# Staging buffers of two kinds, pair sums spread over two groups, and a later start of preparation, in a fused attention and gated-MLP kernel

## The chip, the cores and the metric

The kernel runs on one core of a Trainium2 chip. The metric is the device time of one execution in microseconds (us), and a kernel's time is the median of its runs. The engines are named as in the profile: PE (TensorE, the matrix engine), PEld (its weight loads), DVE (VectorE), ACT (ScalarE), POOL (GpSimd) and SP (SyncE), which here issues nearly all DMAs. Each engine works through its own instructions in a fixed order. A later instruction of the same engine cannot pass one that waits.

## The reference

```python
def _A_ref(x, k_cache, v_cache, wq, wo):          # attention, 32 query heads on 16 K/V heads
    W = min(4096, max(256, Sk // 4))              # 512 cached keys
    q = (x @ wq).reshape(B, Sq, Hq, Dh)...
    k, v = the last W rows of the caches, repeated for 2 query heads
    p = softmax(einsum("bhqd,bhkd->bhqk", q, k) * Dh ** -0.5)
    return einsum("bhqk,bhkd->bhqd", p, v)... @ wo
def _B_ref(x, w1, w3, w2):                        # gated MLP
    return (silu(x @ w1) * (x @ w3)) @ w2
mod = (silu(c) @ w_mod)                           # six vectors sa, ca, ga, sb, cb, gb
h = layernorm(x) * (1 + ca) + sa
x = x + ga * _A_ref(h, ...)
h = layernorm(x) * (1 + cb) + sb
return x + gb * _B_ref(h, ...)
```

There are 2048 rows x of width 576, heads of 128, an MLP width of 4608, and everything is fp32.

## The kernel before, in words

**Precision.** Every operand of a matmul is split into a high part (an ACT cast to the matrix engine's fp32r format, 128 rows wide) and a low part (the difference, taken by POOL or DVE). A product is three matmuls: high x high, high x low, low x high. The helper `split` (lines 84 and 85) does this for most operands.

**Attention** runs in 128 slots. A slot is one head with one block of 512 rows, and has four steps t = 0 to 3. In each step PE gets, in this order: transposes of the previous slot's probabilities (line 335), scores (315 to 317), a part of the next slot's query projection (266, and 274 for the last chunk), the output projection of the slot before the previous one (282). At a slot's end come the value products (351 to 353). Per step ACT makes `p` (line 325) and `pth` (336), DVE `nm` (319), `ptl` (342) and `acc` (366). A query weight `wq` of a head is loaded (`wraw`, line 215), and split into the pair `wh`, `wl` two slots ahead of use. Pairs live in the eight buffers of tag `w`, and serve two slots.

**The MLP** follows in 72 groups, 36 for each pair of row blocks. A group is 7 products (`product`, line 570) of sums of operand blocks, a two-level scheme that does with 7 products what 8 blocks would ask for. They are named p1 to p7 and run in the order p1, p2, p6, p7, p5, p3, p4, steps k = 0 to 6 of a group. Group g belongs to d = g // 2 (d = 0 to 35), j = g % 2. Between the products stand `down` units: 14 for each d, seven a group, run in the two groups after it (`multiply`, line 648; DVE adds each result to its sum, line 636). They use p1 to p7 activations that `act_steps` makes and splits (`split_act`), step by step. The last group but one takes all 14 of d = 34, and d = 35 uses `plain` units (line 658 for the add).

**Preparation.** During attention the MLP weights are turned into what the products read. `load_raw` (471, 474: 12 DMAs) brings blocks of w1 and w3 and `make_set` makes seven sets from them (ACT cast 489, POOL subtracts 490 and 491, store 492). `load_rows` (519: 2 DMAs) and `make_rows` with `keep` (525, 526, 529) do the same for w2, after the gate `b` has been multiplied in (538). Raw blocks stand in the seven buffers of tag `hs`, which four tiles of the normalized input and the modulation matrices use too. A made set (`wmade`, `omade`) stands in one of the four buffers of tag `xn` until its store to DRAM has landed. There are 385 such steps. An order written out by hand places them: `early` steps in slots 8 to 56 and 66 to 74, five for four steps, and the rest in slots 85 to 116. `at(i, t, task)` puts a task into slot i (or group `("m", g)`), and `run(i, t)` issues it there.

**Buffers.** A tag has a fixed number of buffers. A new tile of the tag takes one that is free, the one free for longest, and its first writer waits until the last reader of the old tile has ended.

**Pair sums.** `begin_sums` takes the two buffers of tag `pt` for the sums of a pair. When d = 17 or d = 34 is through, `finish` (lines 592 to 596, five adds of 128x288 for each of four t) folds the sums into the rows of the pair's second block, on POOL. For pair 0 a DVE add (`finish_first`, line 603) does so for the first block. `store_out` (607) then writes rows to `out`. Each of these calls stands right behind the `down` unit that completes its sum.

Of the kernel before, what the change touches and what calls it, by code (L numbers as in the profile page):

```python
# [9 lines left out]
F32R = mybir.dt.float32r  # L10
# [6 lines left out]
P = 128  # L17
D = 576
DC = 4
# [4 lines left out]
ST = SB // P  # L24
# [5 lines left out]
HALF = D // 2  # L30
# [8 lines left out]
def tile_block(  # L39
# [14 lines left out]
    nc = tc.nc  # L54
# [4 lines left out]
    pool = ctx.enter_context(tc.tile_pool(name="pool", bufs=2))  # L59
# [19 lines left out]
    def half_split(a):  # L79
        return a.rearrange("p (a n) -> p a n", a=2)  # L80

    def split(hi, lo, src, eng):

        nc.scalar.copy(hi, src)  # L84
        eng.tensor_sub(lo, src, hi.bitcast(F32))  # L85
# [374 lines left out]

    wdram = {(f, k): dram.tile([P, DC + 1, P], F32, name=f"wd{f}{k}") for f in range(NF) for k in ORDER}
    works = {}

    def load_raw(f):

        whole = pool.tile([P, 6, 3, P], F32, tag="hs", name="wraw", bufs=HB)
        cols = slice(f * P, (f + 1) * P)
        for i, w in enumerate((w1, w3)):
            for k in range(2):
                src = w[2 * k * P : 2 * (k + 1) * P, cols].rearrange("(c p) n -> p c n", p=P)  # L470
                nc.sync.dma_start(whole[:, 2 * i + k, :2, :], src)
            src = w[DC * P :, cols].rearrange("(k r) n -> r k n", k=2)
            for r in range(0, P, 32):
                nc.sync.dma_start(whole[r : r + 32, 2 * i : 2 * i + 2, 2, :], src)  # L474
        works[f] = whole

    def make_set(f, n):


        a11, a12, a21, a22, s1, s2 = (works[f][:, k] for k in range(6))  # L480
        k, x = (("p1", a11), ("p2", a12), ("p4", a22), ("p5", s1), ("p6", s2), ("p7", a21), ("p3", a12))[n]
        if n == 0:
            nc.gpsimd.tensor_add(s1, a21, a22)
            nc.gpsimd.tensor_sub(s2, s1, a11)
        elif n == 2:
            nc.gpsimd.tensor_sub(a21, a11, a21)
            nc.gpsimd.tensor_sub(a12, a12, s2)
        t = pool.tile([P, DC + 1, P], F32R, tag="xn", name="wmade", bufs=ST)
        nc.scalar.copy(t[:, :3, :], x)  # L489
        nc.gpsimd.tensor_sub(t[:, 3:, :], x[:, :2, :], t[:, :2, :].bitcast(F32))  # L490
        nc.gpsimd.tensor_sub(t[DR:, 2, :], x[DR:, 2, :], t[DR:, 2, :].bitcast(F32))
        nc.sync.dma_start(wdram[f, k][:, :, :], t.bitcast(F32))
        if n == 6:
            del works[f]
# [6 lines left out]
    G = NF // 2  # L501
# [19 lines left out]

    def keep(x, to, also=None):

        t = pool.tile([P, 2, HALF], F32R, tag="xn", name="omade", bufs=ST)
        nc.scalar.copy(t[:, 0, :], x)
        nc.gpsimd.tensor_sub(t[:, 1, :], x, t[:, 0, :].bitcast(F32))
        for dst in (to, also):
            if dst is not None:
                nc.sync.dma_start(dst, t.bitcast(F32))
# [47 lines left out]
    def split_act(d, k, x, eng):  # L577
        tags = ("ah", "al") if k in ("p7", "p4", "p6") else ("kv", "kv")
        hi, lo = [pool.tile([P, SB], F32R, tag=t, name=f"a{t}", bufs=8 if t == "kv" else 3) for t in tags]
        split(hi, lo, x, eng)  # L580
        halves[d, k] = hi, lo
# [6 lines left out]
    def finish(pair, t, eng):  # L588

        m15, m6 = msums[pair][0][t], msums[pair][1][t // 2][:, t % 2, :]  # L590
        a = half_split(acc[2 * pair + 1][:, t, :])
        eng.tensor_add(m6, m6, m15[:, 0, :])
        eng.tensor_add(a[:, 1, :], a[:, 1, :], m6)
        eng.tensor_add(a[:, 0, :], a[:, 0, :], a[:, 1, :])
        eng.tensor_add(a[:, 1, :], a[:, 1, :], m15[:, 1, :])
        eng.tensor_add(m15[:, 1, :], m15[:, 1, :], m6)
        if pair == 0:
            store_out(1, t)

    def finish_first(pair, t, eng):  # L600

        a = half_split(acc[2 * pair][:, t, :])
        eng.tensor_add(a, a, msums[pair][0][t])

    def store_out(b, t):
        lo = b * SB + t * P
        nc.sync.dma_start(out[0, lo : lo + P, :], acc[b][:, t, :])
# [3 lines left out]
    def down(d, u):  # L611

        pair = d // G
        lane[0] += 1
        ps = lane[1][lane[0] % 2]
        if u < 4:
            q, t = 0, u
            jobs = [("p4", 0, t), ("p7", 1, t)]
            into = half_split(acc[2 * pair + 1][:, t, :])
        elif u < 6:  # L620
            q, t = 1, u - 4
            jobs = [("p6", 0, 2 * t), ("p6", 0, 2 * t + 1)]
            into = msums[pair][1][t]
        elif u < 10:
            q, t = 2, u - 6
            jobs = [("p1", 0, t), ("p5", 1, t)]
            into = msums[pair][0][t]
        else:
            q, t = 3, u - 10
            jobs = [("p2", 0, t), ("p3", 1, t)]  # L630
            into = half_split(acc[2 * pair][:, t, :])
        multiply(ps, [(halves[d, k], osets[d, q][:, i], r) for k, i, r in jobs])
        if d % G == 0 and q in (1, 2):
            nc.vector.tensor_copy(into, ps[:, :, :HALF])
        else:
            nc.vector.tensor_add(into, ps[:, :, :HALF], into)
        if d == G - 1 or d == 2 * G - 2:
            if q == 2:
                finish(pair, t, nc.gpsimd)
            elif q == 3 and pair == 0:  # L640
                finish_first(0, t, nc.vector)
                store_out(0, t)

    def multiply(ps, jobs):
        for h, ((lh, ll), w, r) in enumerate(jobs):
            rows = slice(r * P, (r + 1) * P)
            for m, (a, b) in enumerate(((lh, 0), (lh, 1), (ll, 0))):
                nc.tensor.matmul(ps[:, h, :HALF], a[:, rows], w[:, b, :], start=m == 0, stop=m == 2)  # L648
# [15 lines left out]
    def act_steps(g, k):  # L664

        d, j = divmod(g, 2)
        x, pool_sub = acts[d], nc.gpsimd.tensor_sub
        if d == 2 * G - 1 and j == 1:
            if k in (0, 1):
                split_act(d, ("p1", "p7")[k], x[0, k], nc.vector)  # L670
            elif k in (5, 6):
                split_act(d, ("p4", "p2")[k - 5], x[1, 6 - k], nc.vector)
        elif j == 0 and d and d - 1 in acts:
            o = acts[d - 1]
            if k == 1:
                split_act(d - 1, "p6", o[0, 0], nc.gpsimd)
            elif k == 2:
                split_act(d - 1, "p5", o[0, 1], nc.gpsimd)
            elif k == 3:
                split_act(d - 1, "p2", o[1, 0], nc.gpsimd)  # L680
                pool_sub(o[1, 0], o[1, 0], o[0, 0])
            elif k == 6 or d == 2 * G - 1 and k == 4:
                split_act(d - 1, "p3", o[1, 0], nc.gpsimd)
                del acts[d - 1]
        elif j == 1:
            if k == 0:
                x["s3"] = pool.tile([P, SB], F32, tag="ql", name="s3", bufs=QB)
                pool_sub(x["s3"], x[0, 0], x[0, 1])
            elif k == 2:
                split_act(d, "p7", x.pop("s3"), nc.gpsimd)  # L690
            elif k == 4:
                split_act(d, "p1", x[0, 0], nc.gpsimd)
            elif k == 5:
                split_act(d, "p4", x[1, 1], nc.vector)
            elif k == 6:
                nc.gpsimd.tensor_add(x[0, 1], x[0, 1], x[1, 1])
                pool_sub(x[0, 0], x[0, 1], x[0, 0])


    AFTER = (1, 1, 1, 1, 2, 0, 1)  # L700
# [3 lines left out]
    def mlp():  # L704

        for g in range(len(groups)):
# [4 lines left out]
            if j == 0:  # L711
                units = iter([(down, d - 1, u) for u in range(14)] if d else ())
            elif d == 2 * G - 1:
                units = iter([(plain, 0, i, t) for i in range(2) for t in range(ST)])
# [42 lines left out]
    def at(i, t, task, *args):  # L757

        tasks.setdefault((i, t), []).append((task, args))
# [31 lines left out]


    last_group = len(groups) - 1
    early = [4 * i + t for lo, hi in ((8, 57), (66, 75)) for i in range(lo, hi) for t in range(ST)]
    late = [4 * i + t for i in range(85, 117) for t in range(ST)]
    items = []
    for p in range(G + 1):
        for f in (2 * p, 2 * p + 1) if p < G else ():
            items += [(load_raw, make_set, f, k) for k in range(7)]
        items += [(load_rows, make_rows, p, k) for k in range(7)]  # L800
# [38 lines left out]
    for pair, i in ((0, 2 * HQ + 23), (1, ("m", 14))):  # L839
        at(i, 0, split_x, pair)  # L840
    at(("m", 2), -1, begin_sums, 0)
    at(("m", 2 * G + 2), -1, begin_sums, 1)

    def begin_h(b):
        hT[b] = new_h()
# [41 lines left out]
    for c in range(3):  # L887
        i = 2 * HQ + 22 + 8 * c
# [141 lines left out]
```

## Time and profile before

| | us |
|---|---|
| median of 3 runs | 3114.67 |
| lowest, highest | 3114.42, 3119.19 |
| profiled execution | 3117.57 |
| its span | 3115.7 |
| mean granted clock of PE in it | 0.995 |

Busy in the profiled execution: PE 3045.8 us (98% of the span), DVE 2000.1, POOL 1634.1, ACT 1479.4. Attention runs up to about 1858 us, the MLP from there. "Idle before" in a row of the profile is what the engine stood idle ahead of that instruction, with what ended the wait. The times of POOL are rough, and matmuls overlap, so that the distance between the starts of two like instructions says more than the busy time.

### The profile page before, as it was taken

What the parts mean: (1) busy time and instruction counts of PE and PEld (TensorE: products, weight loads), DVE (VectorE), ACT (ScalarE), POOL (GpSimd) and SP (SyncE); (2) the same over time, 40 slices, a digit from 0 to 9 for tenths busy, and PEclk for the clock granted to TensorE, in tenths of its full rate; (3) what the DMA queues carried; (4) which work ended last, traced back from release to release, by engine and by line L of the source; (5) the groups of instructions that cost most, each with busy time, mean ns of one, the idle gap of its engine ahead of it and who ended that gap; (6) DMA issues with size and microseconds to landing.
All of it is one profiled execution on the core that took longest, in us unless ns stands there. A gap on an engine that the chain in (4) does not pass through costs nothing.

```text
span 3115.7 us, 47901 instructions
## 1 busy us (share of the span) xinstructions
PE 3045.8 (98%) x16948; PEld 2662.8 (85%) x16948; DVE 2000.1 (64%) x3041; ACT 1479.4 (47%) x3107; POOL 1634.1 (52%) x1657
## 2 busy tenths in 40 slices
PE   7999999999999999999999999999999999999998
PEld 6878888888888888888888888888888888888887
DVE  6766666666777777767777766555555555555555
ACT  5556656655666655566666553333333222322321
POOL 3277877777743752476675113445555453433444
PEclk9999999999999999999999999999999999999999
DMA  4255455545521432245443235667666765666663
GB/s 141 78 170 192 156 187 167 180 167 186 172 76 56 164 119 66 96 170 172 147 161 122 63 139 169 215 227 247 237 232 221 281 223 192 200 206 194 200 204 119
DMA packets 330128, 523.13 MB, mean 168 GB/s; under 512 B 32800, under 2 KB 161824, under 8 KB 328096
## 3 DMA queue, kind: packets, MB, share of 16 engines
q1 hardware_dynamic: 329280, 520.06, 50.2%
q8 instruction: 135, 2.21, 0.3%
q14 instruction: 105, 0.86, 0.1%
q10 hardware_dynamic: 608, 0.00, 0.0%
HBM read 369.76 MB, written 150.18 MB: 167 GB/s over the span
## 4 chain that ended last, share of the span: by engine, by line
PE 77%; POOL 9%; DMA 4%; issue 3%; SPq 3%; DVE 3%; ACT 2%; POOLq 0%; ACTq 0%; DVEq 0%
PE py L570 14%; PE px L570 11%; PE pe L282 9%; PE pq L266 7%; PE pf L648 6%; PE pe L648 6%; PE pt L335 5%; PE po L353 3%; PE po L351 3%; PE po L352 3%; PE pss L317 3%; PE pss L315 3%; PE pss L316 3%; POOL wmade L490 2%; SPq L474 1%
## 5 line engine op out<-in xcount | busy, mean ns | idle before, releaser
L325 ACT ACTIVATE p<-pss,nm 128x512 f32<-128x512 f32 x512 | 352.9, 689 | 341.0 <-DVE nm L319 340.5
L570 PE MATMUL py<-hset,wset 128*128 128x512 f32 x2016 | 507.2, 391 | 2.1 <-DMA wset<-wd0p 2.1
L366 DVE SCALAR_TENSOR_TENSOR acc<-pe,r,acc 128x576 f32<-128x576 f32 x512 | 416.6, 814 | 48.0 <-PE pe L282 42.4
L319 DVE TENSOR_REDUCE nm<-pss 128x1 f32<-128x512 f32 x512 | 349.5, 683 | 111.3 <-PE pss L317 111.2
L570 PEld LDWEIGHTS py<-hset,wset 128*128 128x128 f32 x2016 | 362.9, 188 | 61.2 <-issue 2.6
L342 DVE TENSOR_TENSOR ptl<-pt,pth 128x512 fp32r<-128x512 f32 x512 | 349.5, 683 | 75.1 <-ACT pth L336 74.0
L282 PEld LDWEIGHTS pe<-o,oth 128*128 128x128 f32 x2048 | 326.2, 189 | 71.7 <-DVE acc L366 29.1
L570 PE MATMUL px<-hset,wset 128*128 128x512 f32 x1512 | 382.6, 393 | 0.0
L282 PE MATMUL pe<-o,oth 128*128 128x288 f32 x2048 | 358.4, 297 | 20.4 <-DVE acc L366 19.1
L570 PEld LDWEIGHTS px<-hset,wset 128*128 128x128 f32 x1512 | 277.3, 189 | 49.6
L336 ACT CAST pth<-pt 128x512 fp32r<-128x512 f32 x512 | 300.9, 588 | 30.5 <-PE pt L335 28.1
L335 PE MATMUL pt<-ident,p 128*128 128x128 f32 x2048 | 307.9, 273 | 4.6 <-DVE ptl L342 2.6
L85 POOL TENSOR_TENSOR akv<-u,akv 128x512 fp32r<-128x512 f32 x140 | 179.9, 1295 | 238.5 <-ACT akv L84 237.0
L335 PEld LDWEIGHTS pt<-ident,p 128*128 128x128 f32 x2048 | 249.8, 141 | 18.6 <-issue 3.0
L315 PE MATMUL pss<-kh,qh 128*128 128x512 f32 x512 | 245.2, 479 | 0.7 <-ACT qh L84 0.7
L85 DVE TENSOR_TENSOR otl<-po,oth 128x512 fp32r<-128x512 f32 x128 | 88.6, 692 | 228.6 <-ACT oth L84 228.6
L490 POOL TENSOR_TENSOR wmade<-wraw,wmade 128x256 fp32r<-128x256 f32 x252 | 186.1, 738 | 89.2 <-ACT wmade L489 44.1
L282 PE MATMUL pe<-o,otl 128*128 128x288 f32 x1024 | 219.7, 296 | 0.0
L351 PE MATMUL po<-pth,vh 128*128 128x512 f32 x512 | 203.3, 397 | 11.2 <-ACT pth L336 11.2
L84 ACT CAST oth<-po 128x512 fp32r<-128x512 f32 x128 | 74.9, 585 | 282.1 <-PE po L353 282.1
L353 PE MATMUL po<-ptl,vh 128*128 128x512 f32 x512 | 204.1, 399 | 0.8 <-DVE ptl L342 0.8
L317 PE MATMUL pss<-kh,ql 128*128 128x512 f32 x512 | 203.1, 397 | 0.0
(179 smaller groups left out, 6540.3 us busy)
## 6 DMA issues: line engine op xcount, KB each, us to landing
oset<-od SPq DMA_DIRECT2D x106, 576.0 KB, 4.8
od<-omade SPq DMA_DIRECT2D x133, 288.0 KB, 2.5
oraw<-in_A_wo SPq DMA_DIRECT2D x64, 288.0 KB, 3.1
wraw<-in_B_w SPq DMA_DIRECT2D x144, 128.0 KB, 2.5
wraw<-in_A_wq SPq DMA_DIRECT2D x64, 256.0 KB, 3.2
w2raw<-in_B_w SPq DMA_DIRECT2D x38, 288.0 KB, 3.6
oset<-od SPq DMA_DIRECT2D x35, 288.0 KB, 3.3
wraw<-in_B_w SPq DMA_DIRECT2D x288, 32.0 KB, 1.9
```

The costliest lines, as they stand in the source:

```text
L282: nc.tensor.matmul(E[:, h, :HALF], a[:, rows], b[:, h * HALF : (h + 1) * HALF], start=n == 0, stop=n == 2)
L315: nc.tensor.matmul(pss, st["qh"][:, rows], kh, start=True, stop=False)
L319: nc.vector.tensor_reduce(nm, pss, axis=AX.X, op=ALU.max, negate=True)
L325: nc.scalar.activation(p, pss, AF.Exp, bias=nm, accum_out=st["l"][:, t : t + 1])
L335: nc.tensor.transpose(ps[:, j, :], p[:, j * P : (j + 1) * P], ident)
L336: nc.scalar.copy(st["pt"][0][:, :, t * P : (t + 1) * P], ps)
L342: nc.vector.tensor_sub(pt[1][:, :, cols], state[i]["t"], pt[0][:, :, cols].bitcast(F32))
L351: nc.tensor.matmul(po, vh[:, j, :], pt[0][:, j, :], start=j == 0, stop=False)
L353: nc.tensor.matmul(po, vh[:, j, :], pt[1][:, j, :], start=False, stop=j == KC - 1)
L366: nc.vector.scalar_tensor_tensor(a, E[:, :, :HALF], st["r"][:, t : t + 1], a, op0=ALU.mult, op1=ALU.add)
L570: nc.tensor.matmul(ps, w[:, a, :], h[:, b, :], start=start and n == 0, stop=stop and n == 6, skip_group_check=True)
L648: nc.tensor.matmul(ps[:, h, :HALF], a[:, rows], w[:, b, :], start=m == 0, stop=m == 2)
```

## The change

- A helper `staging` gives made sets a buffer of tag `w` and of tag `xn` by turns; `make_set` and `keep` use it in place of `xn` alone.
- The four `finish` of pair 0 go to steps 0, 2, 4 and 6 of group 37 in place of standing behind their units; `finish_rows` (the DVE add and the store) goes to steps 3 and 5 of group 37 and 0 and 2 of group 38. The four `finish` of pair 1 go to steps 4, 5, 6 of group 70 and 0 of group 71. `begin_sums` of pair 1 moves from before group 38 to its step 3.
- In the last groups the split of p3 is issued at step 3 instead of 4 (before all `finish` of pair 1), the low part of the last p2 split goes from DVE to POOL, and the two adds at the end of group 69 (lines 696 and 697) go from POOL to DVE.
- The early steps of preparation begin at slot 10 instead of 8. Their rate, five sets in four steps, stays; ten more sets fall to the late slots.

```diff
+    staged = [0]
+    def staging(shape, name):
+        staged[0] += 1
+        tag, bufs = (("xn", ST), ("w", 8))[staged[0] % 2]
+        return pool.tile(shape, F32R, tag=tag, name=name, bufs=bufs)
...
-        t = pool.tile([P, DC + 1, P], F32R, tag="xn", name="wmade", bufs=ST)
+        t = staging([P, DC + 1, P], "wmade")
...
-        t = pool.tile([P, 2, HALF], F32R, tag="xn", name="omade", bufs=ST)
+        t = staging([P, 2, HALF], "omade")
...
+    def finish_rows(t):
+        finish_first(0, t, nc.vector)
+        store_out(0, t)
...
-        if d == G - 1 or d == 2 * G - 2:
-            if q == 2:
-                finish(pair, t, nc.gpsimd)
-            elif q == 3 and pair == 0:
-                finish_first(0, t, nc.vector)
-                store_out(0, t)
...
-                split_act(d, ("p4", "p2")[k - 5], x[1, 6 - k], nc.vector)
+                split_act(d, ("p4", "p2")[k - 5], x[1, 6 - k], (nc.vector, nc.gpsimd)[k - 5])
...
-            elif k == 6 or d == 2 * G - 1 and k == 4:
+            if k == (3 if d == 2 * G - 1 else 6):
                 split_act(d - 1, "p3", o[1, 0], nc.gpsimd)
...
-                nc.gpsimd.tensor_add(x[0, 1], x[0, 1], x[1, 1])
-                pool_sub(x[0, 0], x[0, 1], x[0, 0])
+                eng = nc.vector if d == 2 * G - 2 else nc.gpsimd
+                eng.tensor_add(x[0, 1], x[0, 1], x[1, 1])
+                eng.tensor_sub(x[0, 0], x[0, 1], x[0, 0])
...
-    early = [4 * i + t for lo, hi in ((8, 57), (66, 75)) for i in range(lo, hi) for t in range(ST)]
+    early = [4 * i + t for lo, hi in ((10, 57), (66, 75)) for i in range(lo, hi) for t in range(ST)]
...
-    at(("m", 2 * G + 2), -1, begin_sums, 1)
+    at(("m", 2 * G + 2), 3, begin_sums, 1)
+
+    for t in range(ST):
+        at(("m", 2 * G + 1), 2 * t, finish, 0, t, nc.gpsimd)
+        at(("m", 2 * G + 1 + t // 2), (3, 5, 0, 2)[t], finish_rows, t)
+        at(("m", 4 * G - 2 + (t + 1) // 4), (4, 5, 6, 0)[t], finish, 1, t, nc.gpsimd)
```

## The prediction

> **What bounds the kernel now.** I read the page first (busy shares), then windows cut at slot edges, then the waits of ScalarE (ACT) in the stretch that preparation fills, then single waits by chain and timeline. The page:
>
> ```profile
> span 3115.7 us, 47901 instructions
> PE 3045.8 (98%) x16948; PEld 2662.8 (85%) x16948; DVE 2000.1 (64%) x3041; ACT 1479.4 (47%) x3107; POOL 1634.1 (52%) x1657
> ```
>
> TensorE (PE) bounds the kernel, so time is won only where PE waits or runs slow. The change takes no matmul away; all it can win is loss of this kind. To size it I count the score matmuls of line 315 in windows: four of them are one attention slot.
>
> ```profile
> 136.25:152.10 15.85, 1.91 (x4) 0.76 (x4) 1.00 0.19 51
> 165.90:191.70 25.80, 2.21 (x4) 0.91 (x4) 0.87 0.43 147
> 191.70:875.60 683.90, 89.82 (x188) 35.85 (x188) 1.00 0.54 178
> 1004.80:1148.60 143.80, 19.12 (x40) 7.63 (x40) 0.99 0.47 157
> 1277.20:1719.00 441.80, 61.15 (x128) 24.40 (x128) 1.00 0.46 153
> ```
>
> Columns: window, length, PE busy (count), weight loads, granted clock, DMA share, GB/s. The last row is 32 slots at 441.80/32 = 13.81 us, with the late part of preparation in them. Rows three and four are the early part: 47 slots at 14.55 and 10 at 14.38. So the early part loses 683.9 - 47 x 13.81 = 35.0 and 143.8 - 138.1 = 5.7 us. The second row is slot 9 alone, 25.8 us. It also makes a gate on PE, as slot 7 makes a vector (first row, 15.85), so about 10 us of it are loss.
>
> What the early slots wait for, by ACT's waits in 191.7 to 875.6 (us, times, longest); the first and the last of 16 rows on stores (32 waits, 64.4 us in all) and the three other causes beside the slot's own chain:
>
> ```profile
> ACT omade L525 <- DMA od<-omade: 30.9, 14, 5.1
> ACT omade L525 <- DMA wd3p<-wmade: 0.5, 1, 0.5
> ACT omade L525 <- POOL wmade L490: 8.0, 4, 2.1
> ACT o L84 <- POOL oraw L773: 3.5, 2, 1.8
> ACT omade L525 <- POOL omade L526: 1.6, 2, 1.1
> ```
>
> In 1277 to 1719 no such row exists. One wait followed to PE, from the chain:
>
> ```profile
> 543.67 0.45 SPq L519
> 544.24 5.92 DMA wd12p<-wmade
> 550.24 0.12 ACT wmade L489
> 550.65 0.59 ACT pth L336
> 551.27 0.69 DVE ptl L342
> 551.96 0.72 DVE acc L366
> ```
>
> A store, issued behind loads on SP's queue, lands after 5.92 us. Only then may ACT overwrite the buffer. Behind that cast on ACT stands the copy `pth`, behind it VectorE's (DVE) `ptl` and `acc`, and PE waits for `acc`.
>
> **The change, part by part.**
>
> *Staged sets in two kinds of buffers (lines 488 and 524).* No instruction is added. Before, a set reuses the buffer of four sets ago; after, each kind takes every second set, so with four `xn` it is eight sets ago. In `w` eight buffers are shared with `wh`/`wl`, of which at most two pairs are live: four are left at least, again eight sets. Rows for the rate:
>
> ```profile
> L490 POOL TENSOR_TENSOR wmade<-wraw,wmade 128x256 fp32r<-128x256 f32 x158 | 116.7, 739 | 45.0 <-issue 19.9 <-ACT wmade L489 19.7 <-POOL wmade L491 0.7
> L526 POOL TENSOR_TENSOR omade<-w2raw,omade 128x288 fp32r<-128x288 f32 x77 | 61.2, 806 | 57.9 <-ACT omade L525 53.4 <-DMA wraw<-in_B_w 2.7 <-PE pt L335 0.9
> 191.70:875.60 683.90, 662.14 (x3712) 570.70 (x3711) 467.01 (x743) 422.18 (x969) 518.07 (x631) 1.00 0.54 178
> ```
>
> 158 + 77 = 235 sets in 47 slots are 5 a slot. Four more sets of distance are 4/5 x 13.8 = 11 us of grace, against a longest wait of 5.1, so all store waits go. They are 64.4 of the 77.5 us of all these rows (64.4 + 8.0 + 3.5 + 1.6), 83%, so by that share 29 of the 35.0 us. What is late next is GpSimd (POOL). The last row (PE, weight loads, DVE, ACT, POOL) has it busy 518.07 us, and in 649 us without loss that is 80%; `o` then waits for `oraw` as now, or a little more. For that I give back 4: -25. Ends: -35 (all loss), and -6 if POOL's queue takes the stores' place. In 1004.8 to 1148.6 the same share (0.83 x 5.7) gives -4.5, ends 0 and -5.7.
>
> The cover that this needs: a cast into `w` may now wait for a projection (line 274) that read the buffer last. If the pair in use is never handed out, that read is over by more than a slot.
>
> Two of the waits also cost clock. PE's longest wait in 191.7 to 875.6, and the two stretches at half clock there:
>
> ```profile
> PE po L351 <- ACT pth L336: 9.3, 9, 3.0
> 463.60:467.10 3.50, 3.05 (x7) 2.42 (x8) 2.11 (x3) 1.89 (x5) 2.32 (x3) 0.51 0.64 238
> 699.10:702.60 3.50, 3.50 (x11) 2.74 (x10) 1.73 (x3) 1.33 (x4) 2.44 (x4) 0.51 0.68 219
> ```
>
> At clock 0.51 each stretch costs 1.7 us, which lies inside the 35.0 already. The Trainium skill, "TensorE: Matmul & The Clock Gate", section "Part 1: The HAM clock gate (the "warmup" mystery)", lets the clock fall after an idle window of about 3.4 us. By that rule no wait of 3.0 us or less would lower it, the early part would lose 3.4 us less, and the sum would be 3.4 x 0.83 = 2.8 us smaller. The trace does not agree: the clock fell twice here.
>
> *Preparation from slot 10 on.* Loads (12 DMAs a pair of raw blocks, lines 471 and 474; 2 for rows, line 519), casts, subtracts and stores all move by eight steps, on SP, ACT and POOL. What blocked slot 9:
>
> ```profile
> 156.68 1.71 SPq L492 DMA_DIRECT2D wd0p<-wmade  x2
> 171.64 0.81 SPq L519 DMA_DIRECT2D w2raw<-in_B_w  x2
> 169.36 2.22 PE pe L146 x8
> 179.32 0.51 ACT L489 CAST wmade<-wraw 128x384 fp32r<-128x384 f32 x1 [10.28 <-DMA wd0p<-wmade]
> ```
>
> From 158.4 to 171.6 SP stood at the first rows' load: its `hs` buffer (seven; four hold hT, two raw blocks, one the modulation matrix) came free only when the gate was made (line 146, 169.36). Behind it stood the stores, so ACT waited 10.28 us. Two slots later that matrix is gone before the load. Gain 9.5 of the 10; ends -10 and 0 (the pile-up moves onto slots 10 and 11, where eight loads of x stand in SP's queue). Ten sets move to the late slots, 105/32 = 3.3 a slot for 3.0, at the price of the last slot row: 0; if it grew in line to the early part's 0.75 us a slot, 32 x 0.75 x 0.3/2 = +4.
>
> *Pair sums spread (lines 592 to 596, 603).* In groups, seven products of seven matmuls (line 570):
>
> ```profile
> 2492.48:2509.20 16.72, 12.14 (x49) 8.87 (x50) 1.00 0.36 118
> 2509.21:2532.80 23.59, 13.20 (x49) 9.25 (x50) 0.93 0.78 286
> 2509.22 1.29 POOL L85 TENSOR_TENSOR aal<-s,aah 128x512 fp32r<-128x512 f32 x1
> 2515.76 0.79 POOL L596 TENSOR_TENSOR sums<-sums 128x288 f32<-128x288 f32 x1
> 2509.29 1.83 DVE L603 TENSOR_TENSOR acc<-acc,sums 128x576 f32<-128x576 f32 x1 [1.80 <-POOL sums L596]
> ACT s L740 <- POOL aal L85: 5.6, 1, 5.6
> ```
>
> Group 38 loses 6.9 us: `aal` stood behind three of the four finishes, and `s` on ACT waited 5.6 us for its buffer. After, `aal` (k = 2) stands behind one finish and is done about 2502. But all 20 adds stay on POOL, and two 128x512 adds (1.29 us each, as `aal`) that followed the last finish now stand before it, so it ends near 2516.6 + 2.6 = 2519. Until then `finish_rows(3)` waits on DVE, with PE's accumulators behind it, and so does the low half of p6 on POOL, which PE wants after five products and four down units, about 2509.2 + 11 = 2520 (an estimate from 16.72 us for seven of each). I take -3; ends -6.9 and +2. The Trainium skill, "SBUF — State Buffer", section "Who interferes with whom", speaks against more: a DVE instruction with two SBUF inputs contends with GpSimd's reads, so line 603 still meets the adds (here 1.83 us; the trace agrees, and these adds are kept).
>
> *The end (lines 636 to 697).*
>
> ```profile
> 3051.34:3082.79 31.45, 13.79 (x49) 9.79 (x50) 0.89 0.44 150
> 3074.80:3081.60 6.80, 5.53 (x17) 4.86 (x18) 1.98 (x3) 0.00 (x0) 6.41 (x8) 0.50 0.01 2
> PE pf L648 <- POOL akv L85: 4.8, 1, 4.8
> 3064.62 1.30 POOL L681 TENSOR_TENSOR u<-u,u 128x512 f32<-128x512 f32 x1
> 3074.75 1.26 POOL L85 TENSOR_TENSOR akv<-u,akv 128x512 fp32r<-128x512 f32 x1
> 3102.41 0.69 DVE L85 TENSOR_TENSOR akv<-u,akv 128x512 fp32r<-128x512 f32 x1 [0.68 <-ACT akv L84]
> ```
>
> In group 70 the last p3 split (`akv`) stands behind two finishes, and PE waits 4.8 us and then runs 6.8 us at half clock (3.4 lost). After, it follows line 681 directly (3065.9, a cast, 1.26), is done near 3068, and PE asks at 3076.0 - 4.8 = 3071.2: -8.2. The two adds of lines 696 and 697 go to DVE, each as long as its split of the same 128x512, 2 x 0.69 us: between nothing, if they fit DVE's idle time (64% busy on the page), and +1.4; I take +0.5. The last p2 split takes its 0.69 us, and the 0.68 of waiting before it, out of DVE's queue, behind which stand the adds that free PE's accumulators: -0.7, ends 0 and -1.4; the 1.26 us on POOL are covered by the four p4 units that come first. New: finishes run into group 71, past the finish_first adds of POOL there; covered as long as they end before the last eight units. Sum -8.4; ends 0 and -9.6.
>
> **Sum**: -25 - 4.5 - 9.5 - 3 - 8.4 = -50.4. The profiled execution took 3117.57 us (span 3115.7), 2.9 above the median of 3114.67. Its span becomes 3065.3, and the median 3064.3, so 3064.
>
> **The rivals.**
> - POOL takes the stores' place. With ACT no longer held, casts run ahead, and gates and splits of wq and wo sit in POOL's queue (80%). For it: `ACT o <- POOL oraw`; against it: those waits are 3.5 of 77.5 us. Half of the early gain of 29.5 goes: -50 + 15 = -35, 3080.
> - Slower: the shared `w` ring. If sets are given the buffer of the pair still being read, ACT's cast waits for line 274 on PE, once per pair: (47 + 10 + 32)/2 = 44 waits. By the early slots a wait of w on ACT costs 35.0/77.5 = 0.45 w, so 44 cost 20 w. They outweigh the 50 us from w = 2.5 us on; at one step (13.81/4 = 3.45) it is +68 - 50: 3133. Against it: two pairs of eight are live, and a free one is always there.
> - The stores were not held by buffers but by SP's queue, and twice the distance is eaten by a longer queue: only the end, slot 9 and the group remain, -21: 3094. Against it: late slots with 3 sets lose nothing.
> - The end waits anew, for finishes behind a faster PE: the end's 8.4 are lost, 3073.
>
> **How the numbers follow.** My forecast 0.65, with its own range 3053 to 3076; POOL 0.15; the end 0.07; SP's queue 0.05; the ring 0.05; none of it 0.03. The range 3048 to 3090 leaves out the ring, SP's queue and no effect, and reaches near all gains at their best (-35 - 5.7 - 10 - 6.9 - 9.6 = -67). A difference under 0.2% (6 us) cannot be told from none: faster 0.92, same 0.03, slower 0.05.
>
> **What would show it.** Right: rows of ACT waiting for `od` and `wd` gone before 1150, early slots near 13.9, slot 9 near 16, no wait for POOL's `akv` in the last groups, and group 38 below 21. Wrong: ACT casts waiting for PE's `pq`, more waits for POOL's `oraw` and `wl`, or a long slot 10 or 11.

## The result, and the profile after

The changed kernel took 3064.59 us (median of 4 runs, 3063.77 to 3066.29), the kernel before 3114.55 in the same comparison: ratio 0.984 (95% interval 0.982 to 0.985). That is 50 us less, and the forecast was 3064. The profiled execution of the changed kernel took 3066.29 us. In later comparisons the kernel before took 3116 to 3118 us. So each ratio and difference below is against the runs of its own comparison, and stages are compared by their length in the traces.

The head of the page of the changed kernel (lines of its code are 5 to 11 higher than before: products are line 577, the made sets' casts 496 and 532):

```profile
span 3064.5 us, 47936 instructions
PE 3027.4 (99%) x16948; PEld 2654.4 (87%) x16948; DVE 2002.5 (65%) x3042; ACT 1481.7 (48%) x3107; POOL 1635.3 (53%) x1656
```

The number of matmuls is the same. DVE, ACT and POOL are as busy as before within 3 us. PE's busy time falls by 18 us, of which the stretches at half clock explain about 3 (half of PE's busy time in them is 13.7 us before and 10.8 after, those at the start included); the rest has no shown reason, and PE's busy time is modelled. The other 33 of the 51 us were idle time of PE.

The slots after, by windows on the score matmuls (window, length, PE busy (count), weight loads, clock, DMA share, GB/s). The rows are slot 8, slot 9, slots 10 to 56, 66 to 75 and 85 to 116:

```profile
152.48:167.10 14.62, 1.91 (x4) 0.76 (x4) 1.00 0.25 69
167.13:184.35 17.22, 1.91 (x4) 0.76 (x4) 1.00 0.29 92
184.38:840.35 655.97, 90.02 (x188) 35.87 (x188) 1.00 0.55 182
969.60:1108.55 138.95, 19.09 (x40) 7.60 (x40) 1.00 0.48 159
1237.20:1679.40 442.20, 61.09 (x128) 24.32 (x128) 1.00 0.49 162
```

Groups 38, 70, and 71 with the tail, by windows on the products:

```profile
2469.58:2488.66 19.08, 12.15 (x49) 8.83 (x50) 1.00 0.69 234
3007.22:3031.48 24.26, 12.29 (x49) 8.82 (x50) 1.00 0.57 194
3031.50:3064.50 33.00, 12.16 (x49) 8.78 (x49) 1.00 0.19 72
```

| stage | before, us | after, us | difference | forecast |
|---|---|---|---|---|
| slots 8 and 9 | 39.6 | 31.9 | -7.7 | -9.5 |
| slots 10 to 56 | 683.9 | 656.0 | -27.9 | -25 |
| slots 66 to 75 | 143.8 | 139.0 | -4.8 | -4.5 |
| slots 85 to 116 | 441.8 | 442.2 | +0.4 | 0 |
| group 38 | 23.6 | 19.1 | -4.5 | -3 |
| group 70 to the end | 64.3 | 57.3 | -7.1 | -8.4 |

These stages make -51.6 us, and the span fell by 51.2. (The group row: 31.45 + 32.9 before, 24.3 + 33.0 after.)

ACT's waits in slots 10 to 56 of the changed kernel, all but those of the slot's own chain:

```profile
ACT o L84 <- POOL oraw L779: 3.3, 2, 1.6
ACT kh L255 <- PE pt L252: 2.6, 1, 2.6
```

Not one row is left in which ACT waits for a store; before it was 32 waits and 64.4 us. The wait for `oraw` on POOL, which was to be late next, is as long as before (3.5), not longer. The second row is new, and its cause stands in PE's waits and in SP's timeline:

```profile
PE pt L252 <- DMA kvraw<-in_A_k_cache: 2.4, 1, 2.4
286.27 0.98 SPq L478 DMA_DIRECT2D wraw<-in_B_w  x2
291.37 1.96 SPq L481 DMA_DIRECT2D wraw<-in_B_w  x4
293.37 0.43 SPq L239 DMA_DIRECT2D kvraw<-in_A_k_cache  x1
296.90:300.40 3.50, 3.50 (x14) 3.02 (x13) 1.35 (x3) 1.18 (x2) 0.00 (x0) 0.51 1.03 352
```

The load of a head's k stands behind twelve loads of raw weights (the first and the last rows of them are shown), and PE has to wait 2.4 us for it. The last row, a window of all engines, shows that it then ran at clock 0.51. Slots 17 and 18 take 32.1 us for that, where they take 27.8 with the two kinds of buffers alone.

### The profile page after: what moved, and what is told of

Its sections match the earlier page's. It is cut to its first block, busy times and chain, and to the rows that moved or that the text cites. A ratio compares the mean times of both kernels' runs of the same rounds, so it can differ in the third digit from the quotient of the medians.

```text
span 3064.5 us, 47936 instructions
## 1 busy us (share of the span) xinstructions
PE 3027.4 (99%) x16948; PEld 2654.4 (87%) x16948; DVE 2002.5 (65%) x3042; ACT 1481.7 (48%) x3107; POOL 1635.3 (53%) x1656
## 4 chain that ended last, share of the span: by engine, by line
PE 94%; DVE 2%; POOL 2%; ACT 1%; issue 1%; DMA 1%; SPq 0%; ACTq 0%; POOLq 0%; DVEq 0%
PE py L577 15%; PE pe L282 13%; PE px L577 11%; PE pq L266 11%; PE pt L335 7%; PE pf L653 6%; PE pe L653 6%; PE po L353 4%; PE po L352 4%; PE po L351 4%; PE pss L317 4%; PE pss L315 4%; PE pss L316 4%; PE pq L274 2%; PE pt L252 0%
## 5 line engine op out<-in xcount | busy, mean ns | idle before, releaser
L316 PE MATMUL pss<-kl,qh 128*128 128x512 f32 x512 | 202.6, 396 | 0.0
```

The lines of the kernel that those rows point to most:

```text
L316: nc.tensor.matmul(pss, st["qh"][:, rows], kl, start=False, stop=False)
```

## The experiments

### The four parts, each alone on the kernel before

**The two kinds of buffers alone.** The edit is the helper `staging` and its two uses.

> The kernel before with the buffers of two kinds alone; preparation still begins at slot 8, sums and end as before. My theory (a store must land before ACT may write the buffer of four sets ago): no row of ACT waiting for od or wd in the early slots, slots 10 to 56 and 66 to 75 lose 8 us in place of 40.7, so -32; slot 9 keeps its pile-up, because SP still stands at the first rows' load there, and stays above 20 us; groups 38 and 70 stay at 23.6 and 31.4. Time 3082, 3078 to 3088. Rival (SP's queue itself holds the slots, buffers only show it): early slots still lose 25 or more, 3098 or above. Second rival (the buffers alone also cure slot 9): slot 9 near 17, 3073.

Measured: 3076.6 us, ratio 0.9865 (0.985 to 0.988), 41 us less. Slot 9 and slots 10 to 56:

```profile
164.10:183.30 19.20, 1.91 (x4) 0.76 (x4) 1.00 0.48 160
183.35:837.50 654.15, 89.72 (x188) 35.73 (x188) 1.00 0.57 187
```

The loss in slots 10 to 56 falls from 35.0 to 5.3 us, and that in slots 66 to 75 from 5.7 to 0.8. No store wait is left, so the first theory holds and SP's queue as the cause falls. The second rival is half right: slot 9 goes from 25.8 to 19.2 us with no change to when preparation starts. SP still stands as long as before at the load of the first rows:

```profile
154.83 1.71 SPq L499 DMA_DIRECT2D wd0p<-wmade  x2
169.80 0.81 SPq L526 DMA_DIRECT2D w2raw<-in_B_w  x2
```

From about 156.5 to 169.8 it issues nothing, but ACT does not wait for a store there any more (before: 10.28 us). SP's pile-up was real, and most of what it cost PE came through ACT's wait: slot 9 takes 17.2 us where preparation begins later, so 2.0 of 8.6 us are left.

**The later start alone.**

```diff
-    early = [... for lo, hi in ((8, 57), (66, 75)) ...]
+    early = [... for lo, hi in ((10, 57), (66, 75)) ...]
```

> The kernel before with preparation from slot 10 on alone. Theory: slots 8 and 9 fall from 39.6 to about 32 us, -8; store waits stay, early slots still lose 33 to 38, and group 38 and 70 stay. Time 3106, 3102 to 3110. Rival (the pile-up only moves to slots 10 and 11, where loads of x stand on SP): slots 10 and 11 long, time 3112 or more.

Measured: 3100.2 us, ratio 0.994 (0.9925 to 0.9955), 18 us less and so twice what was expected.

```profile
166.70:183.95 17.25, 1.91 (x4) 0.76 (x4) 1.00 0.29 92
183.97:855.50 671.53, 89.73 (x188) 35.73 (x188) 1.00 0.54 177
```

Slots 8 and 9 give the expected 7.7 us. But slots 10 to 56, where just as many sets are made, lose 22.6 in place of 35.0. The store waits fall from 64.4 to 54.3 us in all, less than the loss does.

**The pair sums alone.** The edit is that of the diff for pair 0 and `begin_sums`; pair 1 stays.

> The kernel before with pair 0's sums spread over groups 37 and 38 (and begin_sums of pair 1 at step 3) alone. Theory: group 38 falls from 23.6 to 19.1 us as in the changed kernel, everything else as before. Time 3110, 3108 to 3112. Rival (group 38's gain came from stages ahead of it, by another phase of SP's loads): group 38 stays above 21.5, 3113 or more.

Measured: 3116.1 us, ratio 0.9988 (0.998 to 0.9997). By time it is hardly told from none, and 6 us above what was expected; the stage tells it:

```profile
2511.60:2530.71 19.11, 12.13 (x49) 8.85 (x50) 1.00 0.70 238
PE pf L648 <- POOL aal L85: 0.9, 1, 0.9
PE pe L648 <- DVE acc L640: 0.7, 2, 0.5
```

Group 38 takes 19.1 us, as in the changed kernel. Left over are the two waits that the prediction named: the low half of p6 behind POOL's last finish, and PE's accumulators behind the DVE add that waits for that finish (3.1 us in the changed kernel). In this trace slots 10 to 56 lose 39.3 us, against 35.0 before and 34.7 in the next run, with the same code in all three. So a difference of some 4 us in that stretch, between two traces with store waits, says nothing.

**The end alone.** The edit is that of the diff for pair 1 and the last groups.

> The kernel before with the four edits of the end alone (p3 split before the finishes of pair 1, those finishes later, p2's low part on POOL, two adds on DVE). Theory: group 70 falls from 31.4 to 24.3 us, group 71 to the end stays within 0.5 of 32.9, no half clock near the end. Time 3107.5, 3106 to 3109. Rival (finishes in group 71 cost as much as they free): group 70 falls but the last group grows by 2 or more, 3110.

Measured: 3111.4 us, ratio 0.998 (0.997 to 0.999). Group 70:

```profile
3052.30:3076.50 24.20, 12.32 (x49) 8.80 (x50) 1.00 0.59 195
```

The product window falls from 31.4 to 24.2 us, and the clock in it stays at 1.00. Two expectations were missed. From group 71's start to the end it takes 34.0 us and not 32.9, and there is half clock near the end after all, a stretch of 3.4 us at 3097.1. The edits are not the cause, since the runs without them take 32.9 to 34.5 there. Up to PE's last matmul the last group takes 28.5 to 28.8 us in the traces without such a stretch in it and 29.6 to 29.9 in those with one, with p2's low part on DVE or on POOL.

The four parts alone make -41, -18, -2 and -6.5 us, 67 in all, where together they make 50 and 53 in two comparisons. Two of them win the same time.

### Which two parts overlap

**The changed kernel with preparation from slot 8 again** (`(8, 57)` for `(10, 57)`).

> The changed kernel with preparation from slot 8 again. The two kinds of buffers alone left slot 9 at 19.2 us and slots 10 to 56 with a loss of 5.3; the later start alone took 7.7 us out of slots 8 and 9 and 12.4 out of 10 to 56. Theory now (with eight sets of distance the later start is worth what it leaves of slots 8 and 9, and no more): slots 8 and 9 take 33.1 in place of 31.9 us, slots 10 to 56 lose 5 to 7, time within 2 us of the changed kernel, ratio to before 0.983 to 0.985. Rival (the parts add up, as the prediction had it): 9 us slower than the changed kernel, ratio 0.987.

Measured: 3066.4 us, ratio 0.984 (0.982 to 0.986), the changed kernel's own ratio. Slot 9 and slots 10 to 56:

```profile
165.20:184.00 18.80, 1.91 (x4) 0.76 (x4) 1.00 0.50 164
184.03:838.85 654.82, 89.72 (x188) 35.72 (x188) 1.00 0.57 187
```

The later start wins 0.8 us in slots 8 and 9 and gives 1.2 back behind them (655.97 with it). The wait for a head's k comes with it: from slot 8 the twelve raw loads start at 280.5, 6 us sooner than in the changed kernel, PE does not wait for k, and slots 17 and 18 take 27.8 us. The parts do not add up: with the buffers in place the later start is worth nothing that was measured.

**The kernel before with preparation from slot 12 on alone.**

> The kernel before with preparation from slot 12 on alone. Starting at 10 alone won 20 us: 7.7 in slots 8 and 9, 12.4 in slots 10 to 56, where the rate of sets is the same. Theory (the place of the sets in the four-slot pattern of wq, wo, k and v loads decides how far a store stands back on SP, and 12 has the place of 8): loss per slot in the prepared stretch as from slot 8, 0.75 us, so 12 to 56 lose 30 or more; slots 8 and 9 as from slot 10; time 3106 to 3112, ratio 0.996 to 0.998. Rival (slot 9's pile-up throws the queues back for many slots, and any later start wins the same): 0.5 us a slot or less, 3098, ratio 0.994.

Measured: 3115.7 us, ratio 0.9999 (0.999 to 1.001). Slots 8 and 9, 12 to 56 and 85 to 116:

```profile
149.85:181.74 31.89, 3.82 (x8) 1.52 (x8) 1.00 0.18 57
209.16:862.86 653.70, 85.91 (x180) 34.20 (x180) 0.99 0.52 173
1263.63:1714.79 451.16, 61.09 (x128) 24.32 (x128) 1.00 0.51 169
```

Slots 12 to 56 take 653.7/45 = 14.53 us each: a loss of 0.72 a slot, as from slot 8 (0.75), against 0.48 from slot 10. A backlog from slot 9 is not the reason, since slot 9 is clear here. It fits that the place of the sets in the four-slot pattern of loads decides; only these three starts were tried. The last row was not expected. Twenty sets more than at the start, 115 in 32 slots, make the late slots lose 9.4 us; the 105 of the changed kernel, and of the later start alone, lose 0.4. The time is that of the kernel before, above the range of 3106 to 3112: what slots 8 and 9 win the late slots lose.

### Does the distance count, or the kind?

**The changed kernel with all made sets in `w`.**

```diff
-        tag, bufs = (("xn", ST), ("w", 8))[staged[0] % 2]
+        tag, bufs = ("w", 8)
```

> The changed kernel with every made set in tag w, none in xn. In the built program a set then takes the buffer of the set 4 (185 sets), 5 (3) or 6 (103) before it, and 95 sets take one that wh or wl left; 83 of wh and wl take the buffer of a set 4 or 5 before. Theory (the distance in sets decides): ACT waits for od and wd come back, and early slots (10 to 56) lose 15 to 25 us in place of 7, time 10 to 18 above the changed kernel, ratio 0.987 to 0.9895. Rival (it counts that sets leave the tag that the norm tiles use, not how far apart they are): no waits for stores, as the changed kernel, 0.984. The ring rival of the prediction would show here as ACT casts of sets waiting for PE's line 274.

Measured: 3077.8 us, ratio 0.9874 (0.986 to 0.989). Slots 10 to 56, and the two largest rows of store waits:

```profile
182.90:848.20 665.30, 89.71 (x188) 35.72 (x188) 1.00 0.55 179
ACT omade L532 <- DMA od<-omade: 9.9, 5, 3.2
ACT wmade L496 <- DMA wd12p<-wmade: 4.5, 1, 4.5
```

At a distance of 4 to 6 sets the store waits are back, 28.4 us in all, and the loss is 16.4 us. In the built program of the changed kernel 330 of the 331 sets that follow another set in their buffer stand 8 behind it. Against distance this gives: 4 sets 64.4 us of store waits and 35.0 of loss, 4 to 6 sets 28.4 and 16.4, 8 sets none and 7.1 (5.3 from slot 8). The distance decides, and not that `xn` was left. Though 95 sets take a buffer that `wh` or `wl` left, no cast waits for PE's projections. So the slower rival of the prediction is not there even with all sets in `w`.

### A faster version

**Three edits for what is left in the changed kernel's trace.**

```diff
-            at(i - 3, 0, load, keys, kv, load_kv, k_cache, h // 2)
+            at(i - 4, 3, load, keys, kv, load_kv, k_cache, h // 2)
...
-        at(("m", 2 * G + 1), 2 * t, finish, 0, t, nc.gpsimd)
+        at(("m", 2 * G + 1), 2 * t, finish, 0, t, nc.vector if t == 3 else nc.gpsimd)
...
-                eng = nc.vector if d == 2 * G - 2 else nc.gpsimd
-                eng.tensor_add(x[0, 1], x[0, 1], x[1, 1])
-                eng.tensor_sub(x[0, 0], x[0, 1], x[0, 0])
+                nc.gpsimd.tensor_add(x[0, 1], x[0, 1], x[1, 1])
+                pool_sub(x[0, 0], x[0, 1], x[0, 0])
```

> The changed kernel with three edits for what its trace still shows: the load of a head's k one step earlier (PE waited 2.4 us for it at 294 us, then ran 3.4 us at half clock), the last finish of pair 0 on DVE in place of POOL, and the two adds at the end of group 69 back on POOL. Theory: slots 17 and 18 fall from 32.1 to 27.8, group 38 from 19.1 to 17.5, group 70 from 24.3 to 23.8: 5 to 6 us below the changed kernel, ratio 0.982. Rival (a k tile held longer blocks the three raw buffers, or DVE's five adds hold PE's accumulators): as the changed kernel or above, 0.984 to 0.986.

Measured: 3063.6 us, ratio 0.983 (0.981 to 0.984). Slots 10 to 56, groups 38 and 70, and a wait in group 38:

```profile
181.70:833.37 651.67, 89.72 (x188) 35.72 (x188) 1.00 0.56 183
2462.57:2483.87 21.30, 12.99 (x49) 9.51 (x50) 0.92 0.84 291
3002.43:3026.20 23.77, 12.36 (x49) 8.79 (x50) 1.00 0.58 198
PE pf L653 <- DVE acc L647: 2.3, 1, 2.3
```

The earlier k load takes 4.3 us out of slots 10 to 56 (a loss of 7.1 and 6.7 in two traces of the changed kernel, 2.6 to 2.9 in the three traces with the earlier load), and the two adds back on POOL 0.5 out of group 70, both as expected. Group 38 went the wrong way: five adds on DVE stand before the add that frees PE's accumulator, and two of them took 1.43 us, next to 0.46 for their like, with POOL busy beside them. PE's wait of 2.3 us also cost it a stretch at half clock (0.92 in the window).

**All finishes back on POOL, and two adds ahead of them on DVE.** The k load and group 69 stay as above.

> The changed kernel with the k load one step earlier, and the two adds of lines 702 and 703 on DVE at the end of group 35 (ahead of pair 0's finishes, so that POOL's finishes end 3 us sooner) and on POOL again at the end of group 69; all finishes stay on POOL, since the last one on DVE held PE's accumulators for 2.3 us (group 38 at 21.3). Theory: slots 10 to 56 lose 2.8 in place of 7.1 us, group 70 takes 23.8, group 38 17.5 to 18.5: 5.5 us below the changed kernel. Rival (the adds hold DVE in group 37 as the finish did): group 38 above 19.1, 4 us or less below.

> The changed kernel itself, beside the last version, for the difference between the two: ratio to before 0.984, 4 to 6 us above the other.

Measured: 3063.8 us, ratio 0.9824 (0.981 to 0.984), for this version; 3064.7 and 0.983 (0.982 to 0.984) for the changed kernel beside it. That is 0.8 us below it, where 5.5 had been expected. The two adds had been put with d = 17, whose step lies in group 35, and so group 38 took 19.1 us as in the changed kernel, and the question stayed open. With d = 18, in group 37, against the version before it:

```diff
-                eng = nc.vector if d == G - 1 else nc.gpsimd
+                eng = nc.vector if d == G else nc.gpsimd
```

> As the version before, but with the two DVE adds at the end of group 37 (d = 18), which stand before POOL's last finish; the run before had put them at the end of group 35, so that it did not test this. Theory: POOL's last finish ends 3 us sooner, the low half of p6 is there when PE asks, group 38 falls from 19.1 to 17.5 to 18.3, group 36 back to 16.73; ratio 0.982. Rival (the adds hold DVE, and PE's accumulators with it, as the finish on DVE did): group 38 at 19 or above.

Measured: 3061.4 us, ratio 0.9824 (0.981 to 0.984).

```profile
2464.28:2483.89 19.61, 12.16 (x49) 8.83 (x50) 1.00 0.79 279
PE pe L653 <- DVE acc L647: 2.6, 1, 2.6
```

The rival holds: POOL is no longer awaited in this window, and PE waits 2.6 us for DVE instead. What either engine gives up the other takes over here. Of the three edits the k load and the adds of group 69 are kept by the stages (4.3 and 0.5 us); by times these versions lie 1 to 3 us below the changed kernel, with intervals that overlap, and so no faster version is shown by time.

## Why the prediction was right, point by point

- *Staged sets.* Right in mechanism and size: -32.7 us over both early stretches, forecast -29.5. The 4 us set aside for POOL's queue were not needed: its waits stayed at 3.3 us. The share of 83% was too low, since ACT's waits for POOL's `wmade` and `omade` (9.6 us), which it left in place, went as well; with the k load moved up as well, the stretch loses 2.8 of 35.0. That 27.9 came so close to 25 is in part luck: the wait for k, which was not foreseen, took about the 4 us set aside for another.
- *The clock.* The Trainium skill, "TensorE: Matmul & The Clock Gate", section "Part 1: The HAM clock gate (the "warmup" mystery)", asks for an idle window of about 3.4 us. In the changed kernel the clock fell again after a wait of 2.4 us, so a single wait need not last that long. What the windows have in common stands in the last section.
- *Preparation from slot 10 on.* The stage gave -7.7 for -9.5, but the step failed as an account of the part. It took SP's stand at the `hs` buffer for the cause of slot 9's loss and added it to the gain of the buffers. The runs show that ACT's store wait behind that stand was most of the cost: with the buffers alone slot 9 falls by 6.6 us while SP stands as long. The size was off because slot 9 takes 17.2 us even when it is clear, not the 15.85 of slot 7 to which it was compared, and because slot 8 grows by 0.8. The part is worth 18 us alone and nothing measurable on top. The total came out because the gain was counted once, though under the wrong part.
- *The price of ten more late sets.* 0 was right (+0.4). The bound in line with the early rate (+4) was no bound for the next ten: at 115 late sets, in the kernel before, the price was 9.4 us.
- *Pair sums.* Right, by both waits that were named; -4.5 for -3.
- *The end.* -8.2 for the p3 split and +0.5 for the adds on DVE: group 70 fell by 7.2, and by 0.5 more with the adds back. Both terms are right within 1 us. Of the -0.7 for p2's low part at most 0.3 is to be seen: PE's last matmul comes 28.5 us after group 71's start (28.8 before).
- *What was missed:* the k load behind twelve raw loads (4.3 us). Moving that load up takes the loss away, so SP's order is its cause. It comes with the later start: that part alone has the wait too (1.5 us), and the changed kernel with preparation from slot 8 does not.

## What to carry to other kernels

When a copy on an in-order engine waits for a buffer's store, count how many tiles lie between two uses and multiply by the time a tile takes: that grace against the longest wait tells whether more distance cures it, and idle buffers of another kind can supply the distance. Before gains of several parts are added, follow each loss to the one wait that holds the bounding engine; if two parts take away the same wait, the gain is there once. When loads move in time, look at which other loads they now stand ahead of in the issuing engine's order.

## What was not expected of the hardware

A wait of PE of 2.4 us was enough for a stretch of 3.4 us at half clock, and its length alone does not decide. In group 71 PE has the same wait of 2.4 us in five traces with p2's low part on DVE: the clock fell after it with the later start alone, with the pair sums alone and with the start at slot 12, and did not in the kernel before and with the buffers alone. The clock records show what differs. Within one trace, behind the start of the kernel, the stretches begin whole multiples of 3.41 us apart (before: 463.61, 699.13 and 1101.90). Cut into pieces of 3.41 us on that grid, the 13 traces have 47 pieces at full clock after which it fell. In all of these PE was busy 0.53 of the time or less; of the pieces at full clock, every one under 0.45 was followed by a fall, and none over 0.53. In the changed kernel the piece is this (window, length, then PE, weight loads, DVE, ACT and POOL):

```profile
293.55:296.96 3.41, 1.06 (x7) 0.62 (x6) 0.78 (x2) 0.59 (x1) 0.00 (x0) 1.00 0.72 232
```

PE is busy 1.06 us of 3.41, which is 0.31. In group 71 the wait lies inside one piece where the clock fell (0.31 to 0.37) and is shared by two where it did not (0.73 and 0.49 before).

DVE adds of 128x288 took 0.46 us in one place and 1.43 us, three times as long, in another with POOL at work beside them; in the kernel before, a 128x576 add took 0.76 or 1.83. The two slow adds, and what POOL did beside them (the version with the last finish on DVE):

```profile
2467.34 1.43 DVE L600 TENSOR_TENSOR acc<-acc,sums 128x288 f32<-128x288 f32 x1
2468.80 1.43 DVE L601 TENSOR_TENSOR acc<-acc 128x288 f32<-128x288 f32 x1
2466.89 1.56 POOL L701 TENSOR_TENSOR u<-u,u 128x512 f32<-128x512 f32 x1
2468.53 1.38 POOL L702 TENSOR_TENSOR u<-u,u 128x512 f32<-128x512 f32 x1
```

The Trainium skill, "SBUF — State Buffer", section "Who interferes with whom", says that a DVE instruction with two inputs in SBUF contends with a GpSimd instruction that reads SBUF. That fits these numbers: each slow add began 1.1 us before the end of a POOL instruction and took 0.97 us longer than its like. No run here takes POOL away from beside these two adds.
